# The place of the output copy in VectorE's hand-chained queue

## Chip, cores and metric

The kernel runs on one core of one Trainium2 chip. The metric is the device time of one execution in microseconds (us); the time before is the median of three runs. All other numbers come from the hardware profile of one execution.

## What is computed

Two stages: an agent attention over four sequences of 12480 tokens with 128 channels and 49 agents, and a two-layer network with a squared ReLU on its output. In numpy, cut to its core:

```python
scale = 1.0 / np.sqrt(128)
a2k = softmax(scale * agents @ k.T)       # agents to keys
agent_v = a2k @ v
q2a = softmax(scale * q @ agents.T)       # queries to agents
x = (q2a @ agent_v).reshape(49920, 128)
h = np.maximum(x @ w_in, 0.0)             # w_in: 128 x 2048
out = (h * h) @ w_out                     # w_out: 2048 x 128
```

## The kernel before

**Tiling.** The 49920 tokens are 52 blocks of 960, 13 for each sequence. A block is two groups of 480 tokens. The hidden layer of 2048 is cut into 8 parts of 256; a part for one group of tokens is a *slot*. So a block has 16 slots and the main loop runs over 832 of them, `k`, and four more to drain (`LAG = 4`). Slots are worked on in pairs, an even one and the odd one behind it.

**Front half of a pair** (`first(k)`, at an even `k`). TensorE multiplies the block's attention weights `w` and their remainders `x` with tables that hold the agents' values already multiplied with `w_in`; the results are two tiles `h` in PSUM, one for each slot of the pair, 128 x 2 x 480. They come from a ring of three tiles (`ps_h`), so a pair's second tile takes the place of the pair before's first tile. ScalarE makes the ReLU `r` of both tiles (one buffer, `RB = 1`) and then their square `g_hi` in a reduced precision. VectorE makes the exact square of the even slot, `gg` = r x h; GpSimd subtracts `g_hi` from it, which leaves the low part `g_lo` of the even slot. Then the generator stops at its first `yield`.

The rest of `first` belongs to the odd slot and is resumed at the odd `k`: VectorE makes the exact square in place, in the tile `h` itself (L373 to L375, "odd slot's square"), and subtracts `g_hi` from it, which is the odd slot's `g_lo` ("low part").

**Back half of a slot** (`second(k - 4)`). TensorE adds six matmuls into the accumulator `o`: `g_hi` by the high part of `w_out`, `g_hi` by its low part, `g_lo` by the high part, for two halves each. After the group's 8th part `o` is complete. Then VectorE copies it out of PSUM into `ob`, with a factor, and SyncE issues the DMA to the output. That happens 104 times, twice for each block, always at an odd `k`. `o` has one buffer (`ps_o`, `bufs=1`): the first matmul of the next group writes the tile that the copy reads.

**Order.** Everything of `first` and `second` on TensorE, ScalarE and VectorE goes through `queued`, which chains each instruction behind the one issued before it on the same engine; GpSimd's part is not chained. So VectorE's order around the end of a group is fixed in the source: `gg` of the pair, copy, odd square, odd low part, `gg` of the next pair. TensorE's is: the pair's eight `h` matmuls, twelve `o` matmuls of two older slots, the next pair's `h` matmuls, and so on.

The rest, "background", is placed by the planner between these chained instructions: scores, maxima, values and tables of the next sequence (`background`), and the attention weights of the next block (`queries`: matmuls into `psa`, VectorE's maximum `m`, difference `e` and sum `z`, ScalarE's exponential, GpSimd's products, and transposes by matmul). They use a PSUM tile of their own, `psa`, with one buffer.

In the traces most of the chained instructions carry the line of `queued` (L343); they are told apart by their tiles.

Of the kernel before, what the change touches and what calls it, by code (L numbers as in the profile page):

```python
# [9 lines left out]
F32 = mybir.dt.float32  # L10
# [8 lines left out]
P = 128  # L19
TP = 120  # L20
NT = 8
BLK = TP * NT
G = BLK // 2
# [4 lines left out]
LAG = 4  # L28
# [11 lines left out]
def agent_attention_relu2(ctx: ExitStack, tc: tile.TileContext, qT, kT, v, agT, w_in, w_out, outT):  # L40
    nc = tc.nc
# [5 lines left out]
    NB = N // BLK  # L47
# [29 lines left out]
    for base in (NA, -NA):  # L77
        nc.gpsimd.affine_select(
            out=quad.rearrange("p h a -> p (h a)"), in_=quad.rearrange("p h a -> p (h a)"),
# [55 lines left out]
    state = {}  # L135
# [196 lines left out]
    NP = NCH // 2  # L332
# [7 lines left out]
    def queued(issue, eng, *args, **kw):  # L340

        with tc.issue_after(chain[eng]) if eng in chain else ExitStack():
            ins = issue(*args, **kw)  # L343
        chain[eng] = ins.ins
        return ins

    def first(k):

        g, i = divmod(k, SLOTS)
        j, c = divmod(i, NP)  # L350
        b = g // NB
        w, x = weights[g][j]
        hs = [ps_h.tile([P, 2, 512], F32, name="h") for _ in range(2)]
        outs = [h[:, n, :G] for h in hs for n in range(2)]
        for n, out in enumerate(outs):
            cs = slice((2 * c + n) * P, (2 * c + n + 1) * P)
            queued(nc.tensor.matmul, nc.tensor, out, state[b]["hi"][:, cs], w, start=True, stop=False)

        with tc.high_priority():
            for t, out in enumerate(outs):  # L360
                rows = slice(t * 32, t * 32 + NL)
                queued(nc.tensor.matmul, nc.tensor, out, state[b]["lo"][rows, c // 2, :], x[rows, :], start=False, stop=True)
        r = ffn.tile([P, 2, 2, G], F32, name="r", bufs=RB)
        hi = ffn.tile([P, 2, 2, G], F32R, name="g_hi", bufs=HB)
        gg = ffn.tile([P, 2, G], F32, name="gg", bufs=GB)
        queued(nc.scalar.activation, nc.scalar, r[:, 0], hs[0][:, :, :G], AF.Relu)
        queued(nc.vector.tensor_mul, nc.vector, gg, r[:, 0], hs[0][:, :, :G])
        queued(nc.scalar.activation, nc.scalar, r[:, 1], hs[1][:, :, :G], AF.Relu)
        queued(nc.scalar.activation, nc.scalar, hi, r, AF.Square)
        lo = ffn.tile([P, 2, G], F32R, name="g_lo", bufs=LB)  # L370
        for n in range(2):
            nc.gpsimd.tensor_sub(lo[:, n, :], gg[:, n, :], hi[:, 0, n, :].bitcast(F32))  # L372
        parts[k] = hi[:, 0], lo  # L373
        yield
        queued(nc.vector.tensor_mul, nc.vector, hs[1][:, :, :G], r[:, 1], hs[1][:, :, :G])  # L375
        lo = ffn.tile([P, 2, G], F32R, name="g_lo", bufs=LB)
        queued(nc.vector.tensor_sub, nc.vector, lo, hs[1][:, :, :G], hi[:, 1].bitcast(F32))
        parts[k + 1] = hi[:, 1], lo

    def second(k):  # L380
        g, i = divmod(k, SLOTS)
        j, c = divmod(i, NP)
        hi, lo = parts.pop(k)
        if c == 0:
            acc[0] = ps_o.tile([P, 512], F32, name="o")
        o = acc[0]
        for x in range(3):
            for n in range(2):
                w, y = ((wo_hi, hi), (wo_lo, hi), (wo_hi, lo))[x]
                queued(  # L390
                    nc.tensor.matmul, nc.tensor, o[:, :G], w[:, 2 * c + n, :], y[:, n, :],
                    start=(c == 0 and x == 0 and n == 0), stop=(c == NP - 1 and x == 2 and n == 1),
                )
        if c == NP - 1:
            ob = ffn.tile([P, G], F32, name="ob", bufs=2)
            queued(nc.vector.tensor_scalar_mul, nc.vector, ob, o[:, :G], state[g // NB]["down"])
            t = g * BLK + j * G
            nc.sync.dma_start(outT[:, t : t + G], ob)

    def background(b):  # L400

        kt = load_keys(b, 0, kv, "kt")
        for i in range(NB):
            nxt = load_keys(b, i + 1, kv, "kt") if i + 1 < NB else load_values(b, 0, kv, "vt")
            yield from scores(b, i, kt)
            yield
            kt = nxt
        yield from maxima(b)
        yield
        vt = kt  # L410
        for i in range(NB):
            nxt = load_values(b, i + 1, kv, "vt") if i + 1 < NB else None
            yield from values(b, i, vt, False, nc.gpsimd)
            yield
            vt = nxt
        yield from tables(b)
# [3 lines left out]
    def step(gen):  # L420

        with ExitStack() as es:
            for ins in behind:
                es.enter_context(tc.issue_after(ins))
            return next(gen, "end") != "end"
# [47 lines left out]
    ffn = ctx.enter_context(tc.tile_pool(name="ffn", bufs=4))  # L473
    todo = ahead = iter(())
    for k in range(total + LAG):
        if k < total:
            g, c = divmod(k, SLOTS)
            b, i = divmod(g, NB)
            if i == 0 and c == 0 and b + 1 < B:
                todo = background(b + 1)  # L480
                done = 0
            goal = (i * SLOTS + c + 1) * STEPS / (SPREAD * NB * SLOTS)
            while done < goal and step(todo):
                done += 1
            if c == 0 and g + 1 < B * NB:
                ahead = queries(g + 1)
                step(ahead)
            if c >= 2:
                step(ahead)
            if k % 2 == 0:  # L490
                begun = first(k)
                next(begun)
        if k >= LAG:
            second(k - LAG)
        if k % 2:
            next(begun, None)


# [30 lines left out]
```

## Time and profile before

| | |
|---|---|
| median of 3 runs | 2012.88 us (2011.31 to 2014.65) |
| the profiled execution, its own time | 2016.66 us |
| span of the profile, first to last instruction | 2014.9 us |
| granted TensorE clock, mean of the span | 0.989 |
| ScalarE ReLU `r` | 832 x 971 ns |
| ScalarE square `g_hi` (both slots) | 416 x 1811 ns |
| VectorE `gg` / odd square `h` / odd `g_lo` | 416 each, 1152 / 1155 / 1156 ns |
| GpSimd even `g_lo` | 832 x 1226 ns |
| output DMA `out_T` | 104 x 240 KB |

A row of a timeline has start, duration, engine, line, operation, tiles written and read, shapes and the count of equal instructions merged into it; in square brackets stands the idle time of the engine in front of it and what ended that. PE is TensorE's matmuls, PEld its weight loads, DVE VectorE, ACT ScalarE, POOL GpSimd, SPq SyncE's queue. A group's row ends with busy time, mean ns of one instruction, and the idle time in front of all of them. A row of the waits has the sum in us, the number of times and the longest.

### The profile page before, as it was taken

What the parts mean: (1) busy time and instruction counts of PE and PEld (TensorE: products, weight loads), DVE (VectorE), ACT (ScalarE), POOL (GpSimd) and SP (SyncE); (2) the same over time, 40 slices, a digit from 0 to 9 for tenths busy, and PEclk for the clock granted to TensorE, in tenths of its full rate; (3) what the DMA queues carried; (4) which work ended last, traced back from release to release, by engine and by line L of the source; (5) the groups of instructions that cost most, each with busy time, mean ns of one, the idle gap of its engine ahead of it and who ended that gap; (6) DMA issues with size and microseconds to landing.
All of it is one profiled execution on the core that took longest, in us unless ns stands there. A gap on an engine that the chain in (4) does not pass through costs nothing.

```text
span 2014.9 us, 31143 instructions
## 1 busy us (share of the span) xinstructions
PE 1979.6 (98%) x10980; PEld 1549.3 (77%) x10980; DVE 1682.5 (84%) x1908; ACT 1715.3 (85%) x1700; POOL 1343.0 (67%) x1250
## 2 busy tenths in 40 slices
PE   7799999999999999999999999999999999999999
PEld 7588777777788877777777877777777777777776
DVE  5887888888887888888988788888888888888887
ACT  3477999998887899998887789998888888888887
POOL 2655888875565588886565468886566666666665
PEclk8799999999999999999999999999999999999999
DMA  9633122311122222321112302321011111111100
GB/s 267 152 105 91 45 69 65 79 47 37 44 60 84 71 63 59 81 56 52 40 34 71 93 32 71 79 55 40 29 38 41 33 43 32 44 31 32 39 25 21
DMA packets 99280, 123.42 MB, mean 61 GB/s; under 512 B 7876, under 2 KB 84308, under 8 KB 99124
## 3 DMA queue, kind: packets, MB, share of 16 engines
q1 hardware_dynamic: 99124, 121.43, 22.1%
q8 instruction: 87, 1.43, 0.3%
q14 instruction: 69, 0.57, 0.1%
HBM read 80.97 MB, written 25.56 MB: 53 GB/s over the span
## 4 chain that ended last, share of the span: by engine, by line
PE 90%; DVE 6%; DMA 2%; issue 1%; ACT 1%; POOL 0%; SPq 0%; POOLq 0%; DVEq 0%; ACTq 0%
PE o L343 53%; PE h L343 23%; PE psa L294 4%; PE psa L154 3%; PE psa L211 2%; PE psa L316 2%; DVE gg L343 2%; DVE h L343 1%; DVE g_lo L343 1%; PE h L154 1%; DVE ob L343 1%; DMA kt<-in_kT 1%; DMA ahead<-in_v 1%; DVE e L299 1%; PE h L211 0%
## 5 line engine op out<-in xcount | busy, mean ns | idle before, releaser
L372 POOL TENSOR_TENSOR g_lo<-gg,g_hi 128x480 fp32r<-128x480 f32 x832 | 1001.7, 1226 | 582.6 <-ACT g_hi L343 507.4
L343 ACT ACTIVATE r<-h 128x960 f32<-128x960 f32 x832 | 764.2, 971 | 170.7 <-PE h L343 114.5
L343 ACT ACTIVATE g_hi<-r 128x1920 fp32r<-128x1920 f32 x416 | 753.3, 1811 | 24.9 <-POOL g_lo L372 0.4
L343 DVE TENSOR_TENSOR gg<-r,h 128x960 f32<-128x960 f32 x416 | 479.2, 1152 | 127.8 <-ACT r L343 122.2
L343 DVE TENSOR_TENSOR g_lo<-h,g_hi 128x960 fp32r<-128x960 f32 x416 | 481.0, 1156 | 121.3 <-ACT g_hi L343 101.5
L343 PE MATMUL o<-g_hi,wo_hi 128*128 128x480 f32 x1664 | 537.6, 404 | 0.0
L343 PE MATMUL o<-g_lo,wo_hi 128*128 128x480 f32 x1664 | 496.1, 379 | 0.3 <-POOL g_lo L372 0.3
L343 PE MATMUL o<-g_hi,wo_lo 128*128 128x480 f32 x1664 | 494.7, 378 | 0.0
L343 PE MATMUL h<-w,aw_hi 128*128 128x480 f32 x1664 | 481.4, 397 | 10.1 <-DVE gg L343 8.8
L343 DVE TENSOR_TENSOR h<-r,h 128x960 f32<-128x960 f32 x416 | 480.3, 1155 | 0.3
L343 PEld LDWEIGHTS o<-g_hi,wo_hi 128*128 128x128 f32 x1664 | 280.8, 188 | 107.3 <-issue 54.8
L343 PEld LDWEIGHTS o<-g_lo,wo_hi 128*128 128x128 f32 x1664 | 312.6, 188 | 47.9 <-POOL g_lo L372 0.7
L343 PEld LDWEIGHTS o<-g_hi,wo_lo 128*128 128x128 f32 x1664 | 312.5, 188 | 47.5
L343 PEld LDWEIGHTS h<-w,aw_hi 128*128 128x128 f32 x1664 | 289.6, 189 | 62.3 <-DVE gg L343 23.6
L343 PE MATMUL h<-x,aw_ex 19*128 19x480 f16 x1664 | 161.0, 372 | 0.4 <-DMA aw_ex<-aw_half 0.2
L343 PEld LDWEIGHTS <-aw_ex 19*128 19x128 f16 x1664 | 42.0, 91 | 140.6 <-issue 138.7
L294 PEld LDWEIGHTS psa<-ag,qt 128*120 128x120 f32 x816 | 103.5, 187 | 7.2 <-DVE mx L162 0.4
L343 DVE TENSOR_SCALAR ob<-o,down 128x480 f32<-128x480 f32 x104 | 74.5, 717 | 36.0 <-PE o L343 36.0
L294 PE MATMUL psa<-ag,qt 128*120 128x49 f32 x816 | 98.0, 262 | 0.0
L188 POOL TENSOR_TENSOR vs<-vt,vs 120x1032 fp32r<-120x1032 f32 x39 | 87.0, 2231 | 3.8 <-PE h L343 3.8
L154 PEld LDWEIGHTS psa<-ag,kt 128*120 128x120 f32 x624 | 73.5, 188 | 7.0 <-DMA kt<-in_kT 3.6
L154 PE MATMUL psa<-ag,kt 128*120 128x49 f32 x624 | 72.0, 267 | 3.4 <-DMA kt<-in_kT 3.4
(131 smaller groups left out, 1129.9 us busy)
## 6 DMA issues: line engine op xcount, KB each, us to landing
qt<-in_qT SPq DMA_DIRECT2D x52, 480.0 KB
out_T<-ob SPq DMA_DIRECT2D x104, 240.0 KB
kt<-in_kT SPq DMA_DIRECT2D x39, 480.0 KB
vt<-in_v SPq DMA_DIRECT2D x39, 480.0 KB
x<-half SPq DMA_DIRECT2D x416, 17.8 KB
ahead<-in_kT SPq DMA_DIRECT2D x13, 480.0 KB
ahead<-in_v SPq DMA_DIRECT2D x13, 480.0 KB
w<-w SPq DMA_DIRECT2D x104, 56.2 KB
```

What stands on the lines that cost most here:

```text
L154: nc.tensor.matmul(sv[:, t, :], kt[:, t * TP : (t + 1) * TP], ag[:, b, :], start=True, stop=True)
L188: last[eng] = eng.tensor_sub(out[:, :, n:], x, out[:, :, :n].bitcast(F32))
L211: nc.tensor.matmul(pv[:R, :W], e[:, t, :], vt[:, t, :], start=(t == 0), stop=(t == NT - 1))
L294: nc.tensor.matmul(sv[:, t, :], qt[:, t * TP : (t + 1) * TP], ag[:, b, :], start=True, stop=True)
L299: nc.vector.tensor_sub(e, sv, m.broadcast_to([TP, NT, NA]))
L316: nc.tensor.matmul(pt[:K2, t * TP : (t + 1) * TP], pp[:, j * (NT // 2) + t, :], identr, start=True, stop=True)
L343: ins = issue(*args, **kw)
L372: nc.gpsimd.tensor_sub(lo[:, n, :], gg[:, n, :], hi[:, 0, n, :].bitcast(F32))
```

## The change

The copy and its DMA leave `second` and become a function `out`; `second` now returns what `out` needs when a group is complete. `first` has one more `yield`, between the odd slot's square and its low part. The main loop resumes `first` up to that point, then runs `out`, and then lets `first` end. Nothing else is changed; the number of instructions and their shapes are the same.

```diff
         queued(nc.vector.tensor_mul, nc.vector, hs[1][:, :, :G], r[:, 1], hs[1][:, :, :G])
+        yield
         lo = ffn.tile([P, 2, G], F32R, name="g_lo", bufs=LB)
         queued(nc.vector.tensor_sub, nc.vector, lo, hs[1][:, :, :G], hi[:, 1].bitcast(F32))
...
-        if c == NP - 1:
-            ob = ffn.tile([P, G], F32, name="ob", bufs=2)
-            queued(nc.vector.tensor_scalar_mul, nc.vector, ob, o[:, :G], state[g // NB]["down"])
-            t = g * BLK + j * G
-            nc.sync.dma_start(outT[:, t : t + G], ob)
+        return (g, j, o) if c == NP - 1 else None
+
+    def out(g, j, o):
+        ob = ffn.tile([P, G], F32, name="ob", bufs=2)
+        queued(nc.vector.tensor_scalar_mul, nc.vector, ob, o[:, :G], state[g // NB]["down"])
+        t = g * BLK + j * G
+        nc.sync.dma_start(outT[:, t : t + G], ob)
...
-        if k >= LAG:
-            second(k - LAG)
+        ready = second(k - LAG) if k >= LAG else None
         if k % 2:
+            next(begun, None)
+            if ready:
+                out(*ready)
             next(begun, None)
```

## The prediction

> **What bounds the kernel now.** I read the page's busy times first, then the busy time of a long window, then who waited for whom, then the timelines of TensorE and VectorE around single copies.
>
> ```profile
> span 2014.9 us, 31143 instructions
> ...
> PE 1979.6 (98%) x10980; PEld 1549.3 (77%) x10980; DVE 1682.5 (84%) x1908; ACT 1715.3 (85%) x1700; POOL 1343.0 (67%) x1250
> ...
> L343 DVE TENSOR_SCALAR ob<-o,down 128x480 f32<-128x480 f32 x104 | 74.5, 717 | 36.0 <-PE o L343 36.0
> ```
>
> ```profile
> 500.00:1000.00 500.00, 499.29 (x2794) 391.98 (x2795) 422.31 (x466) 438.58 (x433) 345.09 (x318) 1.00 0.22 61
> ```
>
> ```profile
> PEld h L343 <- DVE gg L343: 20.1, 46, 0.7
> ```
>
> TensorE bounds it: in the main loop it is busy for 499.29 of 500 us at a granted clock of 1.00 (in that row the first number behind the window's length is TensorE's, and the last three are clock, DMA share and GB/s). VectorE waits 36.0 us in front of its 104 copies, but VectorE is not the bound, so these 36 us are not what can be won. Only what stops TensorE counts. The last row (waits from 107 to 2005 us) has what VectorE does to it: 46 times a weight load for the hidden tile h waited on the product gg that frees that tile. That is what can be won; what can be lost is a new wait of TensorE's first o matmul on the later copy, because o has one buffer.
>
> **The change in the rows: a good case.** VectorE, then TensorE, around one copy of a late block:
>
> ```profile
> 1512.13 1.15 DVE L343 TENSOR_TENSOR gg<-r,h 128x960 f32<-128x960 f32 x1 [1.51 <-ACT r L343]
> 1513.80 0.72 DVE L343 TENSOR_SCALAR ob<-o,down 128x480 f32<-128x480 f32 x1 [0.51 <-PE o L343]
> 1514.43 1.15 DVE L343 TENSOR_TENSOR h<-r,h 128x960 f32<-128x960 f32 x1
> 1515.50 0.56 DVE L297 TENSOR_REDUCE m<-psa 120x8 f32<-120x392 f32 x1
> 1515.97 1.15 DVE L343 TENSOR_TENSOR g_lo<-h,g_hi 128x960 fp32r<-128x960 f32 x1
> 1517.04 0.56 DVE L299 TENSOR_TENSOR e<-psa,m 120x392 f32<-120x392 f32 x1
> 1517.51 1.14 DVE L343 TENSOR_TENSOR gg<-r,h 128x960 f32<-128x960 f32 x1
> 1518.57 1.16 DVE L343 TENSOR_TENSOR h<-r,h 128x960 f32<-128x960 f32 x1
> ```
>
> ```profile
> 1513.17 0.60 PE L343 MATMUL o<-g_lo,wo_hi 128*128 128x480 f32 x2
> 1513.60 0.31 PE L294 MATMUL psa<-ag,qt 128*120 128x49 f32 x2
> ...
> 1515.09 0.71 PE L343 MATMUL o<-g_hi,wo_hi 128*128 128x480 f32 x2
> ...
> 1517.80 0.60 PE L343 MATMUL h<-w,aw_hi 128*128 128x480 f32 x2
> 1518.71 0.70 PE L343 MATMUL h<-w,aw_hi 128*128 128x480 f32 x2 [0.31 <-DVE gg L343]
> ```
>
> ```profile
> 1518.71 0.30 PEld L343 LDWEIGHTS h<-w,aw_hi 128*128 128x128 f32 x2 [0.71 <-DVE gg L343]
> ```
>
> Start to start, VectorE's products follow each other after 1.06 us (1517.51 to 1518.57), and a product follows the copy after 0.63 us (1513.80 to 1514.43). Today the first product ends at 1513.28, VectorE idles 0.51 us until the last o matmul ends (1513.17 + 0.60), copies, and does the square h, m, g_lo, e and the next gg without a pause. That gg ends at 1518.65, and at 1518.71 TensorE goes on. What this cost TensorE: two matmuls that follow on each other start 0.22 us apart (0.60 - 0.38, a pair's span less a single one), so the pair after 1517.80 was due at 1518.24; it came 0.47 us late and took 0.70 instead of 0.60, because its weight load was exposed too: 0.59 us with the unrounded times (rounded rows give 0.57).
>
> After the change the square starts at 1513.19, the copy at 1514.25 (o is done since 1513.77, so nothing is waited for), m at 1514.88, g_lo 1515.35, e 1516.42, gg 1516.89: 0.62 us earlier, ending at 1518.04, in time for the load. The 0.59 us are gone. VectorE wins the 0.51 us of idling, and 0.1 us because the copy starts while the square drains. The copy itself costs the same 0.72 us.
>
> Counted over the trace, the copies followed by such a wait: 15 of 0.59 us (545, 1031, and 13 of the late blocks), 3 of 0.34, 3 of 0.39, 6 of 0.09 and 6 of 0.11, all 4.2 to 5.2 us behind a copy; together 8.9 + 1.0 + 1.2 + 0.5 + 0.7 = **12.3 us won**. The other 13 of the 46 come just behind a copy or over 10 us behind one and stay. The 13 late ones have one row (waits from 1500 to 1950 us):
>
> ```profile
> PEld h L343 <- DVE gg L343: 9.4, 13, 0.7
> ```
>
> **The price: TensorE waits for the copy.** With gg first, the copy ends 1.06 + 1.06 + 0.72 = 2.84 us after gg starts, and TensorE may write o some 0.06 us later (gg above ended at 1518.65, the load came at 1518.71): 2.90 to 2.91 us after gg's start. In the case above 1512.13 + 2.91 = 1515.04, and the first o matmul stands at 1515.09: 0.05 us to spare. Where gg is late, it does not fit. VectorE, then TensorE, for the first and the last of nine such copies:
>
> ```profile
> 245.75 1.16 DVE L343 TENSOR_TENSOR gg<-r,h 128x960 f32<-128x960 f32 x1
> 246.82 0.71 DVE L343 TENSOR_SCALAR ob<-o,down 128x480 f32<-128x480 f32 x1
> ...
> 1368.59 1.16 DVE L343 TENSOR_TENSOR gg<-r,h 128x960 f32<-128x960 f32 x1 [1.04 <-ACT r L343]
> ```
>
> ```profile
> 248.00 0.69 PE L343 MATMUL o<-g_hi,wo_hi 128*128 128x480 f32 x2
> ...
> 1369.47 1.04 PE L343 MATMUL h<-w,aw_hi 128*128 128x480 f32 x4
> 1370.44 0.38 PE L343 MATMUL h<-x,aw_ex 19*128 19x480 f16 x4
> 1370.75 0.69 PE L343 MATMUL o<-g_hi,wo_hi 128*128 128x480 f32 x2
> ```
>
> Here VectorE does not idle before the copy, so nothing is won, and the square pushes the copy back: 245.75 + 2.91 - 248.00 = 0.66 us and 1368.59 + 2.91 - 1370.75 = 0.75 us. All nine sum to 6.5 us. Between these and the many with room lie 23 that miss by 0.05 to 0.36 us, the first and the last of them here:
>
> ```profile
> 125.96 1.16 DVE L343 TENSOR_TENSOR gg<-r,h 128x960 f32<-128x960 f32 x1 [0.23 <-ACT r L343]
> ...
> 1995.69 1.15 DVE L343 TENSOR_TENSOR gg<-r,h 128x960 f32<-128x960 f32 x1
> ```
>
> ```profile
> 128.82 0.70 PE L343 MATMUL o<-g_hi,wo_hi 128*128 128x480 f32 x2
> ...
> 1998.44 0.69 PE L343 MATMUL o<-g_hi,wo_hi 128*128 128x480 f32 x2
> ```
>
> They miss by 0.05 and 0.16 us, and all 23 sum to 3.7 us. **Lost: 10.2 us.** The other 71 with a group behind them fit.
>
> **What costs nothing.** The tile view of ob, with the first and the last start:
>
> ```profile
> L343 DVE TENSOR_SCALAR ob<-o,down x104: 707/718/721, 127.4 to 2011.1; 128x480 f32<-128x480 f32 x104
> ```
>
> The copy's output DMA goes out 0.4 to 1.1 us later on SyncE; ob has two buffers and a copy comes every 18 us, (2011.1 - 127.4) / 103; the loads queued behind it fill tiles of the next block. If that cover failed, TensorE would show waits on the operand x. The copy in front of the odd g_lo could hold it up while o is unfinished; but o ends 0.49 us after gg in the good case and the square takes 1.06, so the copy never waits there, and g_lo, read two pairs later, comes earlier. ScalarE's relu, which waits for the square to free r, may start earlier; TensorE gains from that only through gg.
>
> **Sum.** 10.2 - 12.3 = -2.1 us: two effects of opposite sign and nearly one size. The profiled execution took 2016.66 us (1.8 outside its span); it would take 2014.6. The median is 3.8 us below the profiled execution, so I forecast **2010.8 us**, 0.1% less; this kernel's times tell apart about 0.2%, 4 us. Its own range, with the order of the rest kept and the small misses uncertain by 0.1 us each, is 2007.5 to 2014.
>
> **One rule against the trace.** In the good case the load at 1518.71 idled 0.71 us and started with its matmul, though its weights aw_hi do not come from VectorE: the load waits along. The Trainium skill, "TensorE: Matmul & The Clock Gate", section "Step-by-step: what each phase is for", says that TensorE pulls weight loads ahead of matmuls in flight where their row groups do not conflict or the spare weight buffer takes them; the row at 1518.71 does not show it. By it the constant weights of o would be loaded during the new waits, and each of the 32 would be some 0.07 us shorter at most (0.70 less 0.60 is what an exposed load adds, and small misses cannot shrink below nothing).
>
> **Rivals.**
> *The background slips in (slower).* In the good case m stands directly behind the square. If the new order becomes square, m, copy, the copy comes 0.47 us later (1515.50 to 1515.97), and with 0.05 us to spare TensorE waits 0.42 us in each of the 18 blocks with this pattern: +7.6 us, 2018.4 us, slower. It decides from m's place: in front of or behind the copy. For it: m's input psa is done at 1513.91 (1513.60 + 0.31), before the copy's new start. Against it: it was ready before 1514.43 too, and the square went first. 18 in 100.
> *The waits get filled (faster).* Background matmuls are placed where TensorE would stand still. If they move into the nine large waits, those cost nothing, as work merely changes place: -6.5 us, 2004.3 us. For it: such work lies about at copies, as the two psa matmuls at 1513.60. Against it: in front of 1370.75 only h matmuls stand, and none of that work. 22 in 100.
> *Loads pulled ahead.* A load that need not wait for the copy saves up to 32 x 0.07 = 2.2 us: 2008.6 us. The row at 1518.71 speaks against it: 3 in 100.
> *Another order elsewhere (slower).* The instruction order of the background is made anew, and VectorE falls behind at more copies: ten more misses of 0.74 us give 2018.2 us. 10 in 100.
> That the order stays as it was is excluded: square, copy and low part are chained by hand.
>
> **How the numbers follow.** Forecast case 47 in 100, of which 7 fall below 2008.9. Faster by over 0.2%: 7 + 22 + 3 = 32. Slower: 16 of the first rival's 18, and 10: 26. Within: 42. The range runs from the filled waits to the slower rivals with a microsecond around them: 2003.5 to 2019.5.
>
> **What would show it.** Right: the copy's 36 us of idle time nearly gone; the 13 late waits on gg gone; new waits of o loads on ob, about 30, the longest near 0.75 us, some 10 us together; TensorE's busy time almost unchanged. Wrong: m between square and copy, waits on gg that stay although gg comes earlier, or waits on ob that are far more or fewer than 30.

## Result: slower, and the profile after

The changed kernel took 2026.97 us (median of four runs, 2023.55 to 2028.67) beside 2013.77 for the kernel before in the same runs: a ratio of 1.0062, with a 95% interval of 1.0049 to 1.0074, or 12.5 us more. The forecast was 2010.8 us, and the time lies above the whole range.

Three views of the changed kernel follow. First the page: the span, the busy times, the copy's group and the group of the first `o` matmuls.

```profile
span 2024.2 us, 31161 instructions
...
PE 1979.6 (98%) x10980; PEld 1551.4 (77%) x10980; DVE 1680.6 (83%) x1908; ACT 1720.4 (85%) x1700; POOL 1340.7 (66%) x1250
...
L343 PE MATMUL o<-g_hi,wo_hi 128*128 128x480 f32 x1664 | 538.3, 404 | 14.1 <-DVE ob L343 11.2
...
L343 DVE TENSOR_SCALAR ob<-o,down 128x480 f32<-128x480 f32 x104 | 73.9, 710 | 4.9 <-PE o L343 4.9
```

TensorE's busy time is the same to the tenth, 1979.6 us, so no work was added and the whole difference is TensorE standing still (the two profiled executions differ by 9.3 us, 2025.97 against 2016.66; the granted clock was 0.988 against 0.989). The span line has 18 instructions more than before's 31143, so the programs are not equal in number, but of the five engines in the row of busy times every count behind an x is the same. VectorE's idle time in front of its copies fell from 36.0 to 4.9 us, as wanted. In its place stand 11.2 us in which TensorE waits for the copy.

Then the waits of the changed kernel from 107 to 2000 us, the part that the main loop fills (sum in us, number of times, longest):

```profile
PE o L343 <- DVE ob L343: 11.0, 37, 0.8
...
PEld h L343 <- DVE gg L343: 8.9, 20, 0.9
...
PEld o L343 <- DVE ob L343: 5.0, 16, 0.6
...
PE h L343 <- DVE gg L343: 3.9, 8, 0.8
```

And the same two kinds of waits in the late blocks alone, from 1500 to 1950 us, where before had 13 waits of the weight loads on `gg`:

```profile
PE o L343 <- DVE ob L343: 5.9, 23, 0.8
...
PEld h L343 <- DVE gg L343: 0.8, 1, 0.8
```

The 13 waits are gone (the one that is left stands at another place), and there are 23 waits for the copy where before had none. One of them, VectorE's rows and TensorE's around the copy:

```profile
1574.33 1.10 DVE L343 TENSOR_TENSOR gg<-r,h 128x960 f32<-128x960 f32 x1
...
1575.35 1.15 DVE L343 TENSOR_TENSOR h<-r,h 128x960 f32<-128x960 f32 x1
...
1575.66 1.03 PE L343 MATMUL h<-w,aw_hi 128*128 128x480 f32 x4
1576.41 0.71 DVE L343 TENSOR_SCALAR ob<-o,down 128x480 f32<-128x480 f32 x1
...
1576.62 0.38 PE L343 MATMUL h<-x,aw_ex 19*128 19x480 f16 x4
...
1577.27 0.68 PE L343 MATMUL o<-g_hi,wo_hi 128*128 128x480 f32 x2 [0.26 <-DVE ob L343]
```

The order on VectorE is what the source says: `gg`, square, copy. But on TensorE there are only the pair's eight `h` matmuls between the old group and the new one. In the prediction's good case two background matmuls into `psa` stood there as well, and gave the copy its 0.05 us to spare. Their time is still spent, but at another place.

That can be counted over the whole program. Between the last `o` matmul of a group and the first of the next stand, beside `h` matmuls, so often in the 103 cases:

| on TensorE beside `h` | before | after |
|---|---|---|
| four transposes of `pp` | 42 | 26 |
| one or two scores of queries (`ag`,`qt`) | 18 | 6 |
| other background (8 scores, values, tables) | 31 | 33 |
| nothing ("bare") | 12 | 38 |

From start to start (the distance between two neighbouring matmuls less what the same pair takes where nothing is late), the 38 bare copies cost TensorE 15.1 of the 18.5 us that it loses at copies in all. By this measure 54 copies hold it up by more than 0.05 us, where the prediction counted 32. So the first theory, **A**, was: the background was given a new order, and that, not the copy's place, costs the time. Its rivals: **B**, the later copy costs it whatever the order; **C**, the new order is worse by itself; and later **D** and **E**, below.

### The profile page after: what moved, and what is told of

Same layout as the page of the kernel before. It is cut to its first block, busy times and chain, and to the rows that moved or that the text cites. A ratio compares the mean times of both kernels' runs of the same rounds, so it can differ in the third digit from the quotient of the medians.

```text
span 2024.2 us, 31161 instructions
## 1 busy us (share of the span) xinstructions
PE 1979.6 (98%) x10980; PEld 1551.4 (77%) x10980; DVE 1680.6 (83%) x1908; ACT 1720.4 (85%) x1700; POOL 1340.7 (66%) x1250
## 4 chain that ended last, share of the span: by engine, by line
PE 78%; DVE 10%; ACT 7%; issue 2%; DMA 2%; POOL 1%; SPq 0%; DVEq 0%; POOLq 0%; ACTq 0%
PE o L343 45%; PE h L343 20%; PE psa L294 4%; ACT r L343 4%; PE psa L154 3%; DVE h L343 3%; DVE gg L343 3%; ACT g_hi L343 2%; PE psa L211 2%; PE psa L316 2%; DVE g_lo L343 1%; DVE ob L343 1%; PE h L154 1%; PE h L211 1%; DMA kt<-in_kT 1%
## 5 line engine op out<-in xcount | busy, mean ns | idle before, releaser
L343 PE MATMUL o<-g_hi,wo_hi 128*128 128x480 f32 x1664 | 538.3, 404 | 14.1 <-DVE ob L343 11.2
```

## Experiments that leave the order to the planner

In these five the planner makes the background's order anew for each kernel. "Before" was 2015.02 us in the runs of e1 to e4 and 2014.69 in those of e8.

**Only one of a block's two copies moved (e1, e2).** The copies come at slots 3 and 11 of a block.

```diff
             next(begun, None)
+            if ready and k % SLOTS != 3:
+                out(*ready)
+                ready = None
+            next(begun, None)
             if ready:
                 out(*ready)
-            next(begun, None)
```

> The copy stands behind the square only at the groups whose copy falls in slot 3 of a block; at slot 11 it stays between gg and the square. In the programmed order TensorE's background matmuls then keep the places that they have before the change (12 copies with only h matmuls between the groups, as before). Theory A (TensorE waits for the later copy, and how long depends on which matmuls stand between two groups): the rows of before give these 51 copies 16 waits, 4.3 us, and 0.4 us of waits on gg saved: 3.9 us slower than before, about 2017.7. Theory B (the new place of the background does the harm, the copy's wait does not): no change, 2013.8 within 2 us.

It took 2021.97 us, ratio 1.0033 (1.002 to 1.0046) or 6.6 us more, with 12 bare copies: A had said 3.9 and B nothing. From start to start TensorE loses 6.3 us at copies. So the later copy does cost time at this slot, although few copies are bare (the planner moved a few other instructions too), and here nothing is won back: the waits of the weight loads on `gg` stayed at 20.4 us (42 times) from 107 to 2000 us. The waits that can go belong to the other slot's copies. The same with 11 for 3 (e2):

> The reverse: the copy stands behind the square only at slot 11. TensorE's background is placed anew, and 37 copies have only h matmuls in front of the next group (before: 12, changed kernel: 38). Theory A: a copy at slot 3, in the old place, needs no such room, so about half of the changed kernel's waits for the copy remain, 8 to 10 us, and the 11.8 us of waits on gg that fall behind slot 11 are saved: 2010 to 2013. Theory B: the background is as much displaced as in the changed kernel, so the time is near its 2027.

It took 2018.21 us, 1.0017 (1.0008 to 1.0026), between the figures of A and B. It has 37 bare copies, and both sides of the account in one kernel (same window):

```profile
PEld h L343 <- DVE gg L343: 12.5, 34, 0.9
...
PE o L343 <- DVE ob L343: 4.7, 19, 0.7
```

**The copy half a square earlier (e3).** The odd square beside the copy is cut in two, and the copy stands between the halves:

```diff
-        queued(nc.vector.tensor_mul, nc.vector, hs[1][:, :, :G], r[:, 1], hs[1][:, :, :G])
-        yield
+        if c % NP == (LAG - 2) % NP:
+            for n in range(2):
+                queued(nc.vector.tensor_mul, nc.vector, hs[1][:, n, :G], r[:, 1, n], hs[1][:, n, :G])
+                if n == 0:
+                    yield
+        else:
+            queued(nc.vector.tensor_mul, nc.vector, hs[1][:, :, :G], r[:, 1], hs[1][:, :, :G])
+            yield
```

> The odd square of the 104 pairs with a copy is cut into two halves, and the copy stands between them. It then ends 1.06 + 0.56 + 0.72 us after gg starts, 0.5 us earlier than in the changed kernel. 37 copies have only h matmuls behind them. Theory A: of the 18 us of waits for the copy some 3 remain (the late gg only), the waits on gg stay away: 2005 to 2009, faster than both kernels. Theory B: near 2027, because the background stands as in the changed kernel.

2010.44 us, 0.998 (0.9971 to 0.9989): faster than both kernels, if a little over A's 2005 to 2009, though 37 of its copies are bare. So bare copies only cost where the copy is late; half a square less is most of what they miss.

**Background chained behind the copies (e4, e8).** Two steps of `queries` are put into TensorE's hand-made chain, one at each group's end, so that no copy is bare for want of them.

```diff
-            if c >= 2:
+            if c >= 5 and c != 12:
                 step(ahead)
             if k % 2 == 0:
                 begun = first(k)
                 next(begun)
+            if c in (4, 12):
+                pinned[0] = True
+                step(ahead)
+                pinned[0] = False
```

> The changed kernel, but two of the background's steps (scores and second transposes of the next block's queries) are chained into TensorE's order right where it would wait, between the h matmuls and the next group's first o matmul. Only 2 copies are left without background matmuls in front of them (changed kernel: 38). Theory A: under 3 us of waits for the copy are left, so at least 15 us less than the changed kernel unless the chained steps wait themselves: 2003 to 2012. Theory B: no better than the changed kernel, 2024 or more, as the background is displaced even further from its place of before.

2065.78 us, 1.0251 (1.0237 to 1.0265). The stalls at copies did fall, to about 1 us, but the chained matmuls wait themselves, since `psa` has one buffer. The longest rows of TensorE's waits:

```profile
PE psa L291 <- DVE mx L162: 19.2, 9, 3.0
PE psa L291 <- DVE av L220: 9.7, 6, 1.9
```

That says nothing on A. The pair to it, the same chaining with the copy at its old place, came four runs later (e8):

> The kernel before with the same two background steps of each group chained in TensorE's order as in the kernel e4_cover, and the copy at its old place. If the chaining itself cost the 50 us there (its steps waited for the one psum buffer), this one is as slow: 2058 to 2072 us, within 6 us of e4_cover. If the later copy had a part in it beyond the waits seen, it is over 10 us faster than e4_cover.

2070.48 us, 1.0269 (1.0252 to 1.0286): as slow, so the chaining costs the 50 us and the copy's place next to nothing there.

## Experiments that hold the order

What was needed is a kernel in which only the copy moves. In the next ones each instruction of TensorE, ScalarE, VectorE and GpSimd is queued behind the one that precedes it in a given program (issue order only, nobody waits for an instruction to finish). So a program's order can be kept while the copy is put in another place; in short:

```diff
+        for ins, ahead in moved:
+            line.remove(ins)
+            line.insert(line.index(ahead) + 1, ins)
+        for x, y in zip(line, line[1:]):
+            tc.add_manual_dep(y, x.name, ISSUE_ORDER_ONLY)
```

Here `line` is an engine's instructions in the order of the kernel before (or of the changed one), `ins` a copy and `ahead` the odd square behind which it goes. Two orders and two places make four corners; two were measured already. The other two are e5 (old order, new place) and e6 (new order, old place):

> The order in which TensorE, ScalarE and GpSimd run their instructions, and VectorE too, is held to that of the kernel before; only the copy stands behind the odd square instead of in front of it. So the twelve copies with no background matmul behind them stay twelve. Theory A (the slowdown comes from the background work that was placed anew, 38 bare copies instead of 12; the place alone is nearly even): TensorE's waits for the copy 10 to 14 us together, some 32 of them, its weight-load waits on gg down from 20 to 7-10 us, time within -3 to +3 us of the kernel before. Theory B (the later copy itself costs it, whatever the order): 10 to 15 us slower than before.

> The other corner: every engine's order held to that of the changed kernel, with its 38 bare copies, but the copy back in front of the odd square. Theory A: the new order costs only in company with the later copy; the copy then ends some 1.5 us earlier, so the bare groups have room: TensorE's waits for the copy under 2 us together, the gg waits back to 17-22 us, time within -4 to +4 us of before. Theory C (the new order is worse by itself, at any place of the copy): 8 to 15 us slower than before. Theory B (the place alone): as before, and then the run with the old order is slow.

| | copy in front of the square | copy behind the square |
|---|---|---|
| order of before | before: 2014.69 | e5: 2011.79, 0.9982 (0.9974 to 0.9991) |
| order of after | e6: 2021.29, 1.0036 (1.0024 to 1.0049) | after: 2026.97, 1.0062 (1.0049 to 1.0074) |

(The time of after stands beside 2013.77 for before; the ratios are what is compared. In us, a ratio's distance from 1 is taken of 2015.)

With the order of before the change wins 3.6 us (1.8 to 5.2), a little past what A expected, so B falls. With its own order the same move loses some 5 us, and that order costs 7 us (4.8 to 9.9) at the old place too: more than A wanted, and mostly less than C did. In e6 I find five places that before has not, 5.4 us in all from start to start: three waits of 0.95 us on `gg` behind transposes, and two of 1.28 us in front of scores of keys. The rest of its 7 us isn't located. The changed kernel has the same three waits on `gg` (of its loads, 0.92 us each, at 483, 973 and 1464 us); what they come from is shown below.

The waits of e5 from 107 to 2000 us:

```profile
PE o L376 <- DVE ob L431: 5.5, 12, 0.8
...
PEld h L376 <- DVE gg L376: 3.5, 13, 0.7
PEld o L376 <- DVE ob L431: 3.1, 13, 0.3
...
PE h L376 <- DVE gg L376: 0.5, 1, 0.5
```

This is the account of the prediction: few waits on `gg`, some on the copy. In the late blocks (1500 to 1950 us), where after has 23 waits for the copy, e5 has one row:

```profile
PEld o L376 <- DVE ob L431: 0.2, 1, 0.2
```

**Which engine's order counts?** TensorE's matmuls were A's answer. So the changed kernel was run with TensorE's order alone held to that of before (e9):

> The changed kernel with TensorE's order alone held to that of the kernel before; VectorE, ScalarE, GpSimd and the DMA queues come in whatever order they then take. Theory A (what counts is where TensorE's background matmuls stand): as e5_old_order_new_place, 2009 to 2015 us where before is 2014 to 2015, some 40 waits for the copy of 10 to 13 us together. Theory D (it is the order of the other engines, m's place on VectorE among them, that costs): 2018 us or more.

2027.87 us, 1.0065 (1.0052 to 1.0078): theory A, as it was put, is wrong, and D's bound holds. TensorE has its 12 bare copies, and fewer waits for the copy than e5; but the waits on `gg` are back, more than before had. The rows of e9 (107 to 2000 us):

```profile
PEld h L377 <- DVE gg L377: 23.3, 38, 1.6
...
PE h L377 <- DVE gg L377: 11.6, 19, 1.2
...
PE o L377 <- DVE ob L377: 3.0, 8, 0.8
```

and before's second row in the same window, whose first is the prediction's (20.1 us, 46 times):

```profile
PE h L343 <- DVE gg L343: 5.9, 19, 0.5
```

What VectorE does differently is seen in a late block of e9, VectorE, GpSimd and the matmuls for `h`:

```profile
1598.57 2.42 POOL L406 TENSOR_TENSOR g_lo<-gg,g_hi 128x480 fp32r<-128x480 f32 x2 [2.06 <-ACT g_hi L377]
...
1598.74 1.15 DVE L377 TENSOR_TENSOR g_lo<-h,g_hi 128x960 fp32r<-128x960 f32 x1
...
1599.80 1.21 DVE L339 TENSOR_SCALAR z<-z 120x8 f32<-120x8 f32 x1
...
1600.93 1.14 DVE L377 TENSOR_TENSOR gg<-r,h 128x960 f32<-128x960 f32 x1
1601.01 0.60 PE L377 MATMUL h<-w,aw_hi 128*128 128x480 f32 x2
...
1602.13 0.70 PE L377 MATMUL h<-w,aw_hi 128*128 128x480 f32 x2 [0.52 <-DVE gg L377]
```

and in the same block of e5:

```profile
1588.71 1.15 DVE L376 TENSOR_TENSOR gg<-r,h 128x960 f32<-128x960 f32 x1
...
1589.77 0.16 DVE L337 TENSOR_SCALAR z<-z 120x8 f32<-120x8 f32 x1
1589.85 1.16 DVE L376 TENSOR_TENSOR h<-r,h 128x960 f32<-128x960 f32 x1
...
1590.91 0.20 DVE L338 RECIPROCAL z<-z 120x8 f32<-120x8 f32 x1
...
1591.01 2.42 POOL L405 TENSOR_TENSOR g_lo<-gg,g_hi 128x480 fp32r<-128x480 f32 x2 [1.62 <-PE h L376]
```

The addition of 1e-9 to the sum `z`, eight numbers on 120 partitions, takes 0.16 us in e5, where GpSimd pauses. In e9 it stands in front of `gg` and takes 1.21 us; it ends at 1601.01, 0.02 us behind GpSimd's two subtractions (1598.57 + 2.42 = 1600.99). `gg` comes a microsecond late, and TensorE waits 0.52 us. The tile view of `z` shows how often (shortest, middle and longest duration in ns; e5, e9, after):

```profile
L337 DVE TENSOR_SCALAR z<-z x52: 150/171/1179, 41.2 to 1932.7; 120x8 f32<-120x8 f32 x52
```

```profile
L339 DVE TENSOR_SCALAR z<-z x52: 152/878/1214, 42.6 to 1950.2; 120x8 f32<-120x8 f32 x52
```

```profile
L305 DVE TENSOR_SCALAR z<-z x52: 152/171/1184, 42.8 to 1921.6; 120x8 f32<-120x8 f32 x52
```

In e9 the middle one is long: 27 take 0.88 us or more. In after 14 take 0.95 or more; before has 12 of 0.75 to 1.18 us. That GpSimd holds VectorE up is what the ends show: all 27 in e9 and all 14 in after end 0.02 to 0.04 us behind an instruction of GpSimd. The Trainium skill, "SBUF — State Buffer", section "Who interferes with whom", says of what: VectorE and GpSimd share a pair of ports, a `tensor_scalar` on SBUF operands can take it, and whoever comes second waits for the whole instruction of the other. The rows agree to 0.02 us; no run here tried the ports by themselves. Theory **E**: this addition costs the time, where the new order sets it beside GpSimd's work and in front of a `gg` (so it is with 15 of the 27 in e9; in after 9 of the 14 stand between the copy and the odd `g_lo`). Four kernels (e11 to e14) leave the addition out and hold the rest in place.

```diff
         nc.vector.reduce_sum(z, e, axis=AX.X)
-        nc.vector.tensor_scalar_add(z, z, 1e-9)
         nc.vector.reciprocal(z, z)
```

> Leaves out the addition of 1e-9 to the softmax sum z (51 small VectorE instructions); every engine's order is held to that of e9_tensor_order_only otherwise. There, 27 of these additions took 0.9 to 1.2 us instead of 0.16, each ending 0.03 us behind the end of a GpSimd instruction, 13 of them late, directly in front of a gg. Theory E (these are what makes e9 slow though TensorE's order is the old one): VectorE is free some 19 us sooner in all, the thirteen late weight-load waits of 0.67 us go or fall under 0.2, and the time falls by 8 to 16 us, to 2012 to 2020. If they are only a symptom: 2025 to 2029 as e9.

> The changed kernel, its order held, without the addition of 1e-9 to z. There 14 of the additions took 0.95 to 1.2 us. Theory E with A (both have a part: the bare copies the larger, 15 us of waits of TensorE that stay): 2 to 6 us under the changed kernel, 2021 to 2025, with the waits for the copy as before (11 us by the page, 18 us from start to start). If z has nothing to do with it in the changed kernel: 2026 to 2028. If it is all z: under 2018.

> A control for the three others: the kernel before, its order held, without the addition of 1e-9 to z. 12 of the additions waited for GpSimd in before, 8 us of VectorE time in all with the instructions themselves, 13 more stand between the gg and the square (0.16 us) and are in front of no late gg. Theory E: 0 to 4 us under before. If leaving out z's addition is worth as much here as in e11, it says nothing on the order.

| order, copy's place | with the addition | without it |
|---|---|---|
| e9's order (TensorE's of before), behind | 1.0065 (1.0052 to 1.0078) | e11: 2012.1, 0.9983 (0.9975 to 0.9992) |
| after's order, behind | 1.0062 (1.0049 to 1.0074) | e12: 2019.87, 1.0021 (1.0012 to 1.003) |
| before's order, in front | 1 | e14: 2014.16, 0.9994 (0.9985 to 1.0003) |

E holds: leaving the additions out is worth 16.5 us (0.0082 of 2015) in e9's order, 8.3 in the changed kernel (2 to 6 were expected), and 1.2 in the order of before, which can't be told from nothing. No run holds the changed kernel's order without another change; that holding costs nothing by itself is seen in e14 only, for the order of before. In e11 the waits on `gg` went with them (107 to 2000 us):

```profile
PEld h L377 <- DVE gg L377: 4.5, 18, 0.7
...
PE o L377 <- DVE ob L377: 2.9, 8, 0.8
...
PE h L377 <- DVE gg L377: 0.6, 1, 0.6
```

And what is left in e12, the changed kernel without the addition:

```profile
PE o L377 <- DVE ob L377: 10.8, 37, 0.8
...
PEld o L377 <- DVE ob L377: 5.3, 18, 0.6
...
PEld h L377 <- DVE gg L377: 4.1, 13, 1.2
...
PE h L377 <- DVE gg L377: 1.1, 1, 1.1
```

Neither kernel has the additions; e11 has 12 bare copies and e12 has 38. From start to start TensorE loses 18.5 us at copies in e12 and 9.1 in e11, 9.4 us apart (in the first rows alone, 10.8 and 2.9, it is 7.9), and the two times differ by 0.0038 of 2015, 7.7 us. That is A's part, with the limit that the other engines' orders differ between the two as well.

So the 12.5 us are made up of **-3.6** for the move with the order kept (e5), **+8.3** for the additions at their new places (after against e12), and **+7.7** for the copies left bare (e12 against e11): 12.4, each of the three uncertain by some 2 to 3 us either way. The step between, from e5 to e11, is 0.2 us; it leaves the additions out and changes the order of VectorE, ScalarE and GpSimd. Of the 8.3 us the profiles show a part only: from their first `h` matmul to the end after and e12 differ by 5.4 us. TensorE's own waits on `gg` fall from 3.9 to 1.1 us, its loads' from 8.9 to 4.1. Which of the 51 additions cost the rest isn't located.

The addition isn't the only small instruction that is held. Three times in the main loop VectorE multiplies `rl` with `up`, 98 numbers. The first of the three in after, then in e12:

```profile
478.72 1.04 DVE L261 TENSOR_TENSOR rl<-rl,up 98x1 f32<-98x1 f32 x1
```

```profile
480.02 0.15 DVE L296 TENSOR_TENSOR rl<-rl,up 98x1 f32<-98x1 f32 x1
```

In after it ends 0.02 us behind a subtraction of GpSimd, and starts 3.4 us after an addition of 1.13 us (475.30); the wait of 0.92 us at 483 follows. All three are held in after, e6 and e9, and none in e11 and e12, where the three waits are gone as well (before holds them too, 1.13 us each, but has no such wait behind them). So the 8.3 and 16.5 us are what leaving the addition out did in all, and not the sum of the additions' own delays.

**A version that beats both (e7).** The order of before, and the copy between the two halves of the square:

> Order held to that of the kernel before; the odd square beside the copy is cut in two halves and the copy stands between them. Theory A: both of the two waits are small at once (for the copy under 3 us together, on gg 8 to 13 us), and 7 to 12 us are won against before: 2003 to 2008 us where before is 2015. If the order matters little for this place, it is the time of the half-square kernel with its own order, 4 to 5 us under before.

2004.95 us, 0.9951 (0.9937 to 0.9964): 9.9 us faster than before and 22 faster than the change. Both kinds of waits are small at once (107 to 2000 us):

```profile
PEld h L376 <- DVE gg L376: 7.4, 31, 0.7
...
PE o L376 <- DVE ob L437: 1.6, 6, 0.3
```

Its control (e10) has the halves but the copy in front of them:

> A control for e7_old_order_half: order held to that of the kernel before, the copy at its old place in front of the odd square, and the square beside it cut in two halves behind it. Theory A: the halves bring nothing by themselves, the gain of e7 comes from the copy standing between them; gg waits stay at 20 to 27 us, and the time is 0 to 6 us above before for the added instruction. If the cut itself lets TensorE's weight loads go sooner, it is 3 us or more under before.

2020.47 us, 1.0031 (1.002 to 1.0043), a little over what was expected; the loads' waits on `gg` are 24.3 us (45 times). So the halves cost time by themselves, and the gain comes from the copy's place between them. And e13, e7 without the addition to `z`:

> The kernel e7_old_order_half (order of before, square cut in halves, copy between) without the addition of 1e-9 to z. In the order of before 11 or 12 of the additions waited for GpSimd (0.65 us more each), few of them in front of a gg. Theory E: 0 to 4 us under e7, so 2001 to 2005.

2004.54 us, 0.9946 (0.9934 to 0.9958), which can't be told from e7: in the order of before the additions stand where they do little or no harm.

## Why the prediction was wrong

Taken step by step, against after and against e5, where the order was kept:

- **What bounds.** Right. TensorE's busy time stayed, and all of the change is in its waits.
- **12.3 us won.** Right in e5: the distances between neighbouring `h` matmuls lost 12.2 us against before, and no late wait on `gg` is left. In after the 13 late ones went too, but the new order put others elsewhere.
- **10.2 us lost in 32 waits.** Nearly right in e5: 11.3 us from start to start. The ruler was too short for most. It let TensorE go on 0.06 us behind the copy; in the row at 1577.27 it goes on 0.15 us behind it (1576.41 + 0.71 = 1577.12), and so it does in the nine large waits of e5, which are 0.68 to 0.85 us in place of 0.66 to 0.75; some of those that fitted miss by a few hundredths. In others (14 in after) 0.05 us is right.
- **The sum, -2.1 us, "with the order of the rest kept".** e5 gives -3.6 (-5.2 to -1.8): right for the case that it describes.
- **The step that failed** is the one that took this case for the real one: "The other 71 with a group behind them fit." They fit by the background matmuls that stood there in before's trace. Those have no fixed place; the planner set them anew when the copy moved, and 26 copies more became bare. In the same way "what costs nothing" looked at what is queued by hand on VectorE and not at the small instructions of the background between them, whose place moved as well. The addition to `z` stood between `gg` and the square 18 times in before and 3 times in after; between the copy and the odd `g_lo` it stood 9 times in after, held up each time, and never in before. Leaving it out is worth 1.2 us in the one order and 8.3 in the other.
- **Rivals.** "Another order elsewhere" was the right one, with 10 in 100 and a price of ten misses of 0.74 us (it came to more than twice that, from two causes of which one was not thought of). "The background slips in" did not happen as it was put: `m` stayed behind the copy. `z`'s sum came between square and copy 9 times and the maximum `mx` twice, and none of these copies cost TensorE anything. "The waits get filled" went the other way: cover was taken from the waits.
- **The rule on weight loads.** The row of TensorE's loads at the longest kind of new wait shows the load held with its matmul; the bracket names ScalarE, whose `g_hi` the matmul needs too, but the copy ended last, at 304.31 (after):

```profile
303.60 0.71 DVE L343 TENSOR_SCALAR ob<-o,down 128x480 f32<-128x480 f32 x1
...
304.42 0.30 PEld L343 LDWEIGHTS o<-g_hi,wo_hi 128*128 128x128 f32 x2 [1.02 <-ACT g_hi L343]
304.45 0.68 PE L343 MATMUL o<-g_hi,wo_hi 128*128 128x480 f32 x2 [0.77 <-ACT g_hi L343]
```

The weights are constants and the load still came 0.11 us behind the copy's end. In the 14 that went on 0.05 us behind the copy, the load started with its matmul. So the rival that had loads pulled ahead finds no support here.

What stays open: why the planner left the copies bare. The runs show what its order costs, not how it came about.

## What to carry to other kernels

Where a planner orders part of the work, a row of the trace that "fits" does so by the work that stands beside it, and that work moves when a hand-made chain changes. So price an edit twice, with the order kept and with the cover gone, and give the second case the weight that the slack deserves (0.05 us to spare is none). To test which it is, hold every engine's order and move the one instruction: here that turned 0.6% slower into 0.2% faster, and showed the way to 0.5%.

## What the runs showed of the hardware

- A VectorE `tensor_scalar` of 120 x 8 numbers takes 0.15 to 0.2 us with GpSimd idle or between two instructions, and up to 1.21 us beside GpSimd's subtraction of 1.2 us; it then ends 0.02 to 0.04 us behind GpSimd (after, e5, e9). The product `rl` of 98 numbers took 0.15 us free and 1.04 to 1.06 us held (e12; after, e9). The reciprocal of the same eight numbers as the addition's took 0.18 to 0.20 us everywhere in these traces, also where GpSimd worked throughout (30 of 52 in after).
- TensorE's first matmul into a PSUM bank came 0.14 to 0.15 us behind the end of VectorE's copy out of it where its load was 0.03 us ahead of it (rows at 304.45 and 1577.27), and 0.05 us behind it where load and matmul started together (14 times in after). Behind the end of `gg` it was 0.05 to 0.06 us (before, after). What makes the one or the other isn't shown.
- A square cut in two costs 6 us for 103 cuts where nothing else is gained (e10), about 0.06 us each.
